# One buffer for a unit's attention data, own output tiles for the W1 jobs, and new ticks for the background jobs

## Chip, core and metric

The kernel runs on one core of one Trainium2 chip. The metric is the device time of one execution in microseconds (us). Before the change three executions took 1047.87, 1049.3 and 1052.65 us; the median is 1049.3 us.

## What is computed

```python
# chunked attention, 4 x 8 heads, 768 tokens, 64 wide; a chunk of 32 queries sees
# 8 memory keys, 16 keys to the left, its own 32 and 8 to the right
out = softmax(q_c @ k_full.T / 8) @ v_full
x = out.transpose(0, 2, 1, 3).reshape(3072, 512)
h = x @ w_in1;  x = (maximum(h, 0) + log1p(exp(-abs(h)))) @ w_out1    # 512 -> 2048 -> 512
h = x @ w_in2;  y = (h - tanh(h)) @ w_out2                            # 512 -> 2048 -> 512
```

All is float32. The kernel splits a float32 operand into a high and a low part and makes three matmuls of one product.

## The kernel before

Tokens come in 24 attention units of 128 and in six blocks of 512. The program has four stages.

1. Opening (to about 125 us). The first weights arrive, units 0 to 7 of the attention and block 0 of the first feed-forward layer run, in an order written out by hand in `OPENING`. There a token such as `L9` loads the score data (`qk`) and values (`v`) of unit 9.
2. Plain blocks (to about 431 us). Blocks 1 to 3 of layer 1 run as products `ff_h` and `ff_y` of twelve matmuls each, 2.72 us a product. After each product `tick()` is called once (L877), and a tick number is the clock of all background work. At the ticks of `ATT_TICKS` (five or six ticks apart) TensorE does, for neighbouring units, the transposes of one (`t_mm`), the value product of the one before (`v_mm`, L371) and the scores of the next (`s_mm`, L290). One tick later (r == 1) SyncE gets the loads of a unit.
3. Phase 0 (ticks 98 to 153, to about 588 us). The last two blocks of layer 1 together, as a fast (Strassen-like) product: seven products in place of eight.
4. Phases 1 to 3, the same form for layer 2. Each phase has an h part of 56 products of six matmuls (1.36 us each; a tick after every second one) and a y part.

In an h part, two lanes alternate: product n belongs to weight group p = 0 or 1 for n = 0 to 13, to p = 2 or 3 for n = 14 to 27, and so on. The weights of a group come from DRAM in a first half (four products, 1024 KB) and a second half (three products, 768 KB), through a ring of five slots (`Ring`, loads at L699). A slot is loaded again once TensorE has made its last product from it, so the load for the second lane's first half (p = 3, 5, 7) can start at the end of n = 6, 20, 34 and is needed at n = 15, 29, 43.

Beside these products run background jobs, started at ticks by tables:

- `JOBS_W1` (16 jobs, `job_w1`): sums of the layer-1 weights for phase 0. A job started at tick t copies the high part on ScalarE at t+2 (L468), stores it at t+3 (`put`, L477), makes the low part on VectorE at t+3 (L472) and stores it at t+4. Each store is 512 KB. The two parts stand in tiles named `o`, a pool of four that is shared with the W2 jobs, the plain output (`out1`, L462) and the x2 jobs.
- `JOBS_W2` (16 jobs (tick, slot, lead), `job_w`): one load of 1024 KB of raw layer-2 weights, and after the lead and four steps of decoding the stores, 768 KB at lead+5 and lead+6 and 1024 KB at lead+8 and lead+9. The first eight are the input weights, the last eight the output weights.
- `JOBS_X` (`job_x`): layer-2 input for the four phases from the layer-1 output: one load of 1024 KB and seven products' inputs, 512 KB each, stored at lead+2 to lead+7.

Every DMA is issued by SyncE in program order. Its queue waits at an instruction whose data, slot or semaphore isn't ready, and all later DMAs wait behind it. `defer` puts a store at the beginning of a later tick, ahead of that tick's attention loads.

Attention tiles `qk` (768 KB) and `v` (512 KB) have two buffers each: at a unit's r == 1 the scores' data of the unit after next are loaded, and the values of the unit itself, which `v_mm` reads two boundaries later.

Of the kernel before, what the change touches and what calls it, by code (L numbers as in the profile page):

```python
# [8 lines left out]
F32 = mybir.dt.float32  # L9
F32R = mybir.dt.float32r  # L10
# [8 lines left out]
B, H, S, D = 4, 8, 768, 64  # L19
NMEM = 8  # L20
CHUNK, LEFT, RIGHT = 32, 16, 8
KEYS = NMEM + LEFT + CHUNK + RIGHT
P = 128
NCH = P // CHUNK
NPAIR = H // 2
# [13 lines left out]
ATT_ORDER = (8, 9, 10, 11, 20, 12, 13, 14, 15, 21, 16, 17, 18, 22, 19, 23)  # L39
ATT_TICKS = (0, 6, 11, 16, 21, 26, 31, 37, 42, 47, 53, 58, 63, 69, 74, 79, 84, 90)  # L40
AT_END = ATT_TICKS[-1]
VIA_DRAM = (20, 21)

# [11 lines left out]
h10 K0 y13 l10 K3 V4 s11 H10 L6 xh4 c47 h11 S5 s13 c19 Y6 K4 mx5 h13 l11 c38 h12 K5 c48 H11 xl4 c110  # L55
l12 c39 K6 y14 l13 ex5 H12 s14 K7 Y7 ml5 c49 T5 c310 Y8 y15 c410 pT5 s15 K8 h14 c111 V5 S6 L7 l14
c311 H13 xh5 h15 mx6 c112 l15 c411 K9 H14 xl5 ex6 c113 K10 Y9 ml6 K11 T6 H15 pT6 c312 c412 K12 V6 S7
xh6 L8 Y10 mx7 ex7 c114 ml7 K13 Y11 xl6 K14 T7 c314 Y12 c313 pT7 c413 c115 V7 Y13 xh7 L9 c315 xl7
c414 c415 K15
"""  # L60
ORDER = "qk0 qk1 qk2 qk3 v0 v1 i0 v2 v3 o0 w1 w2 w3 qk4 v4 w4 w5 w6 w7 qk5 v5 w8 w9 w10 w11 w12 w13 w14 w15"
# [11 lines left out]
HALF = 2 * P  # L73
# [5 lines left out]
AHEAD = 3  # L79
GSLOT = (8, 9, 10, 11, 12, 13, 14, 7)  # L80
JOBS_W1 = (
    (0, "o", 7), (4, "i", 7), (8, "o", 6), (12, "i", 6), (16, "o", 0), (20, "i", 0), (24, "o", 1), (29, "i", 1),
    (35, "o", 2), (40, "i", 2), (44, "o", 3), (48, "i", 3), (52, "o", 4), (61, "i", 4), (70, "o", 5), (75, "i", 5),
)
JOBS_W2 = (
    (5, 15, 3), (17, 15, 3), (23, 6, 3), (31, 15, 3), (38, 6, 3), (46, 15, 3), (51, 6, 3), (60, 15, 3),
    (67, 6, 3), (73, 15, 3), (90, 10, 4), (96, 15, 4), (105, 14, 5), (112, 15, 5), (127, 15, 4), (148, 15, 4),
)
JOBS_X = (
# [3 lines left out]
)  # L93
JOBS_X1 = (79, 91)
# [9 lines left out]
def attention_ffn_ffn(  # L104
# [18 lines left out]
    opool = ctx.enter_context(tc.tile_pool(name="o", bufs=4))  # L123
    attention = ExitStack()
    apool = attention.enter_context(tc.tile_pool(name="a", bufs=2))
# [16 lines left out]
    wid1 = [dpool.tile([P, 7, 2, HALF], F32, name=f"wid1{p}") for p in range(NP)]  # L142
    x1d = dpool.tile([P, KT, len(VIA_DRAM) * P], F32, name="x1d")

# [76 lines left out]
    def run(steps):  # L221
        for _ in steps:
            pass
# [9 lines left out]
    att = {}  # L233

    def qk_load(u):
        t = apool.tile([P, NPAIR * (P + NCH * KEYS)], F32, name="qk")
        nc.sync.dma_start(out=t, in_=qk[u])
        q = t[:, : NPAIR * P].rearrange("p (a t) -> p a t", a=NPAIR)
        k = t[:, NPAIR * P :].rearrange("p (c a k) -> p c a k", c=NCH, a=NPAIR)
        att[u] = dict(q=q, k=k)  # L240
# [16 lines left out]
            nc.scalar.copy(out=out, in_=q)  # L257

    def v_load(u, v=None):
        v = apool.tile([P, NCH, NPAIR, D], F32, name="v") if v is None else v  # L260
        nc.sync.dma_start(out=v.rearrange("p c a d -> p (c a d)"), in_=vv[u])
        att[u]["v"] = v

    def at_load(u):
        qk_load(u)
        v_load(u)
# [72 lines left out]
    def t_mm(u, ps):  # L339
        a = att[u]  # L340
        for p in range(NPAIR):
            nc.tensor.transpose(  # L342
                ps[:, p * P : (p + 1) * P], a["sm"][:, p * P : (p + 1) * P], ident
            )
        a["t"] = ps

    def t_out(u):
        a = att[u]
        if u < UB:
            pT = early[:, UB + u].rearrange("p (a t) -> p a t", a=NPAIR)  # L350
        else:
            pT = apool.tile([P, NPAIR, P], F32, name="pT", bufs=1)
        a["pT"] = pT
        nc.scalar.copy(out=pT.rearrange("p a t -> p (a t)"), in_=a.pop("t"))
# [22 lines left out]
    def x_whole():  # L377
        if "whole" not in xt:
            xt["whole"] = xpool.tile([P, 2, KT, N], F32, name=f"x{PLAIN % 2}")
            n = len(VIA_DRAM) * P  # L380
            nc.sync.dma_start(out=xt["whole"][:, 1, :, :n], in_=x1d)
        return xt["whole"]

    def x_out_whole(u):
        src = att.pop(u)["x"]
        o = (u % UB) * P
        if u in VIA_DRAM:
            x = apool.tile([P, 2 * NPAIR * KEYS], F32, name="sm").rearrange("p (k t) -> p k t", k=KT)
# [3 lines left out]
        yield  # L392
        if u in VIA_DRAM:
            yield
# [68 lines left out]
            nc.vector.tensor_copy(out=o[:, 1], in_=ps_y[e + 2][:, :N])  # L463
            defer(nc.sync.dma_start, y1d[j // 2][e][:, j % 2], o, more=1)

    def split_to(src, dst, shape):
        hi = opool.tile([P, *shape], F32R, name="o")
        nc.scalar.copy(out=hi, in_=src)  # L468
        yield
        put(hi, dst(0))  # L470
        lo = opool.tile([P, *shape], F32R, name="o")
        nc.vector.tensor_tensor(out=lo, in0=src, in1=hi.bitcast(F32), op=ALU.subtract)  # L472
        defer(put, lo, dst(1))

    def put(t, places):
        for at, n, place in places:
            nc.sync.dma_start(out=place, in_=t[:, at : at + n].bitcast(F32))  # L477

    def job_w(kind, p, slot, lead):
# [20 lines left out]
        def place(s, a, n):  # L500
            return wid[p][:, a : a + n, s] if kind == "i" else wod[1][:, a : a + n, p, s]

        yield from split_to(
            w[:, 1:4], lambda s: ((0, 2, place(s, 0, 2)), (2, 1, place(s, 6, 1))), [3, HALF]
        )
        sums(w)
        yield
        yield
        yield from split_to(w, lambda s: ((0, 4, place(s, 2, 4)),), [4, HALF])

    def sums(w, order=(0, 1)):
        add, sub = ALU.add, ALU.subtract
        i, j = order
        nc.vector.tensor_tensor(out=w[:, i], in0=w[:, i], in1=w[:, 3], op=add)
        nc.vector.tensor_tensor(out=w[:, j], in0=w[:, i], in1=w[:, j], op=sub)
        nc.vector.tensor_tensor(
            out=w[:, 2:4], in0=w[:, 2:4], in1=w[:, j : j + 1].to_broadcast([P, 2, HALF]), op=sub
        )
# [11 lines left out]
    def job_w1(kind, p):  # L530
        c = tpool.tile([P, 4, HALF], F32, name="c2", bufs=1)
        a, b = (
            weights["slot", f][:, "io".index(kind)].bitcast(F32).rearrange("p s (i n) -> p i s n", i=2)
            for f in (p, p + NP)
        )
        if kind == "o":
            parts = (c[:, 0:2], a), (c[:, 2:4], b)
        else:
            parts = (c[:, 1:3], a), (c[:, 0:4:3], b)
        for out, x in parts:  # L540
            nc.vector.tensor_tensor(out=out, in0=x[:, :, 0], in1=x[:, :, 1], op=ALU.add)
        yield
        sums(c, (1, 0) if kind == "o" else (0, 1))
        yield

        def place(s):
            return wod[0][:, 2:6, p, s] if kind == "o" else wid1[p][:, 2:6, s]

        yield from split_to(c, lambda s: ((0, 4, place(s)),), [4, HALF])

    def job_x1(half):
        cols = slice(half * N // 2, (half + 1) * N // 2)
# [309 lines left out]
    for t, kind, p in JOBS_W1:  # L862
        plan.setdefault(t, []).append(lambda x=(kind, p): job_w1(*x))
# [7 lines left out]
    place = [0, 0]  # L871
    soft = {}

    def defer(f, *args, more=0):
        late.append((now[0] + more, f, args))

    def tick(chain=iter(())):  # L877
        k = now[0]
        now[0] += 1
        calls, late[:] = [x for x in late if x[0] <= k], [x for x in late if x[0] > k]  # L880
        for _, f, args in calls:
            f(*args)
        if k in starts:
            place[:] = starts[k], k
        i, r = place[0], k - place[1]
        u, done, last = (ATT_ORDER[j] if 0 <= j < len(ATT_ORDER) else None for j in (i, i - 1, i - 2))
        if r == 1 and u is not None:
            if i + 2 < len(ATT_ORDER):
                qk_load(ATT_ORDER[i + 2])
            if i > 1:  # L890
                v_load(u)
            next(soft[u])
        if r == 2 and u is not None:
            run(soft.pop(u))
        if r == 1 and last in VIA_DRAM:
            run(soft.pop(("x", last)))
        if r == 0:
            if done is not None:
                t_mm(done, ps_h[(k // 2 + 1 + k % 2) % 2])
            if last is not None:  # L900
                v_mm(last, ps_a)
            if u is not None:
                s_mm(u, ps_a)
        next(chain, None)
        if r == 0 and done is not None:
            t_out(done)
        next(chain, None)
        if r == 0 and last is not None:
            soft["x", last] = (x_out if last // UB < PLAIN else x_out_whole)(last)
            next(soft["x", last])  # L910
        if r == 0 and u is not None:
            soft[u] = softmax(u)
            next(soft[u])
        if r == 0 and last is not None:
            next(soft["x", last], None)
        run(chain)
        active.extend(job() for job in plan.get(k, ()))
        for job in active[:]:
            if next(job, active) is active:
                active.remove(job)  # L920

    with tc.manual_schedule(engines={mybir.EngineType.PE}):
# [10 lines left out]
        if True:  # L933
# [6 lines left out]
            for name in ORDER.split():  # L940
                kind, i = name.rstrip("0123456789"), int(name.lstrip("qkviow"))
# [23 lines left out]
            for token in OPENING.split():  # L965
                op = token[:2] if token[0] == "c" else token.rstrip("0123456789")
                i = int(token[len(op) :])
# [156 lines left out]
```

## Time and profile before

| | |
|---|---|
| runs, median | 1049.3 us |
| profiled execution | 1051.89 us, its span 1050.1 us |
| TensorE (PE) | 1036.8 us busy, 7327 matmuls |
| VectorE (DVE), ScalarE (ACT) | 766.0 and 620.1 us busy |
| DMA | 319.99 MB, mean 305 GB/s |

The span runs from the first to the last instruction. Busy time of an engine is a sum over the whole span; where TensorE waits, only the waits on it and the chain that ended last can say why.

### The profile page before, as it was taken

The numbers are of one execution on the slowest core, as the hardware profiler recorded it, in microseconds if no ns is written. First come the engines' busy times: TensorE is split into PE (matmuls) and PEld (weight loads), VectorE is DVE, ScalarE is ACT, GpSimd is POOL, SyncE is SP. The second block draws the span as 40 slices with busy tenths as digits, with TensorE's granted clock in tenths as the row PEclk, the third lists the DMA queues.
The fourth block names the chain that finished last, engine by engine and source line by source line (L and its number), as shares of the span: only waits on it lengthen the run. The fifth ranks groups of instructions, "written<-read, shape, count | busy, mean of one in ns | idle before, by whom it ended". The sixth has DMA issues, their size and how long they took to land.

```text
span 1050.1 us, 18534 instructions
## 1 busy us (share of the span) xinstructions
PE 1036.8 (99%) x7327; PEld 848.5 (81%) x7327; DVE 766.0 (73%) x1168; ACT 620.1 (59%) x968; POOL 7.9 (1%) x14
## 2 busy tenths in 40 slices
PE   8999999999999999999999999999999999999998
PEld 5778888888888888877888888888888888888886
DVE  6998467787886774774698687778477777446876
ACT  6998556676675765665664565545455554444553
POOL 2000000000000000000000000000000000000000
PEclk9999999999999999999999999999999999999999
DMA  9989976989898977999999999888799889655661
GB/s 376 407 320 339 294 270 203 318 292 363 296 348 279 340 247 254 376 382 381 331 388 357 341 360 381 303 321 314 264 354 340 320 305 327 213 176 208 239 201 61
DMA packets 112663, 319.99 MB, mean 305 GB/s; under 512 B 8512, under 2 KB 67392, under 8 KB 94144
## 3 DMA queue, kind: packets, MB, share of 16 engines
q1 hardware_dynamic: 112576, 318.80, 84.7%
q8 instruction: 58, 0.95, 0.3%
q14 instruction: 29, 0.24, 0.1%
HBM read 220.73 MB, written 98.04 MB: 304 GB/s over the span
## 4 chain that ended last, share of the span: by engine, by line
PE 88%; DMA 6%; DVE 3%; ACT 2%; issue 1%; SPq 0%; ACTq 0%; DVEq 0%
PE ps_y L408 43%; PE ps_h L408 28%; PE ps_b L408 14%; DMA w<-in_w1i 2%; PE ps_a L371 2%; PE ps_a L290 1%; DMA x<-wid 1%; DMA wod<-o 1%; DMA qk<-in_qk 1%; DVE gl L727 1%; DMA w<-in_qk 1%; PE ps_h L342 1%; DMA wid<-o 1%; DVE o L196 0%; DVE w L727 0%
## 5 line engine op out<-in xcount | busy, mean ns | idle before, releaser
L790 ACT CAST gh<-w 128x512 fp32r<-128x512 f32 x224 | 139.4, 623 | 137.3 <-DVE gl L727 106.8
L727 DVE TENSOR_TENSOR gl<-w,gh 128x512 fp32r<-128x512 f32 x239 | 164.5, 690 | 63.1 <-ACT gh L790 57.0
L408 PE MATMUL ps_h<-x,w 128*128 128x512 f32 x720 | 175.4, 393 | 0.6 <-DVE w L205 0.3
L408 PE MATMUL ps_y<-gh,w 128*128 128x512 f32 x512 | 169.9, 393 | 0.2 <-ACT o L462 0.2
L408 PEld LDWEIGHTS ps_h<-x,w 128*128 128x128 f32 x720 | 133.8, 188 | 31.2 <-DVE w L205 1.5
L408 PE MATMUL ps_y<-w,x 128*128 128x512 f32 x552 | 129.3, 389 | 0.0
L408 PEld LDWEIGHTS ps_y<-w,x 128*128 128x128 f32 x552 | 103.6, 188 | 21.5
L408 PEld LDWEIGHTS ps_y<-gh,w 128*128 128x128 f32 x512 | 96.1, 188 | 21.6 <-ACT o L462 0.6
L408 PE MATMUL ps_y<-gh,x 128*128 128x512 f32 x352 | 109.2, 389 | 0.0
L408 PE MATMUL ps_y<-gl,w 128*128 128x512 f32 x256 | 99.8, 390 | 0.0
L449 DVE TENSOR_TENSOR gl<-t,gh 128x512 fp32r<-128x512 f32 x64 | 45.5, 714 | 52.0 <-ACT gh L444 51.9
L754 ACT ACTIVATE tanh<-sum 128x512 f32<-128x512 f32 x72 | 45.4, 632 | 60.7 <-DVE sum L723 60.5
L408 PEld LDWEIGHTS ps_y<-gh,x 128*128 128x128 f32 x352 | 66.1, 188 | 13.7
L408 PE MATMUL ps_b<-w,x 128*128 128x512 f32 x276 | 71.3, 394 | 0.0
L408 PE MATMUL ps_h<-gh,x 128*128 128x512 f32 x176 | 68.5, 389 | 0.0
L408 PE MATMUL ps_b<-gh,x 128*128 128x512 f32 x176 | 68.5, 389 | 0.0
L408 PE MATMUL ps_y<-gl,x 128*128 128x512 f32 x176 | 68.5, 389 | 0.0
L408 PE MATMUL ps_h<-w,x 128*128 128x512 f32 x252 | 64.5, 391 | 3.0 <-DMA x<-wid 3.0
L432 ACT ACTIVATE t<-ps_h 128x512 f32<-128x512 f32 x64 | 38.1, 597 | 47.7 <-PE ps_h L408 46.8
L727 DVE TENSOR_TENSOR w<-w 128x512 f32<-128x512 f32 x88 | 60.3, 687 | 2.4 <-ACT w L432 1.3
L408 PEld LDWEIGHTS ps_b<-w,x 128*128 128x128 f32 x276 | 52.6, 191 | 11.1
L723 DVE TENSOR_TENSOR sum<-ps_y,kept 128x512 f32<-128x512 f32 x48 | 32.9, 690 | 37.5 <-PE ps_y L408 29.2
(167 smaller groups left out, 1675.3 us busy)
## 6 DMA issues: line engine op xcount, KB each, us to landing
x<-wod SPq DMA_DIRECT2D x44, 1024.0 KB, 5.0
x<-wid SPq DMA_DIRECT2D x27, 1024.0 KB, 7.7
w<-x2d SPq DMA_DIRECT2D x21, 1024.0 KB, 7.3
x<-wid SPq DMA_DIRECT2D x24, 768.0 KB, 7.2
wod<-o SPq DMA_DIRECT2D x32, 512.0 KB, 7.2
wid<-o SPq DMA_DIRECT2D x32, 512.0 KB, 5.7
qk<-in_qk SPq DMA_DIRECT2D x21, 768.0 KB, 6.6
ring<-wod SPq DMA_DIRECT2D x12, 1024.0 KB, 6.6
```

The source lines that it names most:

```text
L290: nc.tensor.matmul(out=ps[cc, j, KEYS * p : KEYS * (p + 1)], lhsT=a["q"][r, p, cc], rhs=a["k"][r, c, p, :], start=True, stop=True,)
L342: nc.tensor.transpose(ps[:, p * P : (p + 1) * P], a["sm"][:, p * P : (p + 1) * P], ident)
L371: nc.tensor.matmul(out=ps[h : h + 64, p % 2, 2 * P + t0 : 2 * P + t0 + CHUNK], lhsT=v, rhs=pT, start=True, stop=True,)
L408: nc.tensor.matmul(out=ps, lhsT=a, rhs=b, start=first and i == 0, stop=last and i == 2, skip_group_check=on,)
L432: nc.scalar.activation(out=out, in_=x, func=AF.Softplus)
L449: eng.tensor_tensor(out=gl, in0=t, in1=gh.bitcast(F32), op=ALU.subtract)
L723: nc.vector.tensor_tensor(out=h, in0=ps, in1=t, op=ALU.add)
L727: nc.vector.tensor_tensor(out=out, in0=x, in1=y, op=ALU.subtract)
L754: nc.scalar.activation(out=t, in_=h, func=AF.Tanh)
L790: nc.scalar.copy(out=gh, in_=src)
```

## The change

The attention tiles lose their second buffer. Units 1, 5 and 7 of the opening use the tiles `oa` and `ob`; all other units use the one `qk` and the one `v`. The loads move one unit nearer to their use: at r == 1 of a unit, the scores' data of the next unit and the values of the unit before. `L9` leaves the opening. When attention's `oa` and `ob` are free (after unit 7), they are the two output tiles of the W1 jobs, which then use none of the four `o` tiles. The three tables get new ticks, slots and leads.

```diff
+AHEAD_UNITS = (1, 5, 7)
-xh6 L8 Y10 ... Y13 xh7 L9 c315 xl7
+xh6 L8 Y10 ... Y13 xh7 c315 xl7
 JOBS_W1 = (
-    (0, "o", 7), (4, "i", 7), (8, "o", 6), (12, "i", 6), (16, "o", 0), (20, "i", 0), (24, "o", 1), (29, "i", 1),
-    (35, "o", 2), (40, "i", 2), (44, "o", 3), (48, "i", 3), (52, "o", 4), (61, "i", 4), (70, "o", 5), (75, "i", 5),
+    (0, "o", 7), (4, "i", 7), (8, "o", 6), (12, "i", 6), (18, "o", 0), (22, "i", 0), (27, "o", 1), (31, "i", 1),
+    (35, "o", 2), (39, "i", 2), (43, "o", 3), (53, "i", 3), (59, "o", 4), (65, "i", 4), (70, "o", 5), (74, "i", 5),
 )
 JOBS_W2 = (
-    (5, 15, 3), (17, 15, 3), (23, 6, 3), (31, 15, 3), (38, 6, 3), (46, 15, 3), (51, 6, 3), (60, 15, 3),
-    (67, 6, 3), (73, 15, 3), (90, 10, 4), (96, 15, 4), (105, 14, 5), (112, 15, 5), (127, 15, 4), (148, 15, 4),
+    (6, 15, 3), (18, 15, 3), (23, 6, 3), (30, 15, 3), (37, 6, 3), (42, 15, 3), (50, 6, 3), (55, 15, 3),
+    (64, 6, 3), (71, 15, 3), (90, 10, 4), (97, 14, 4), (105, 7, 5), (115, 15, 5), (141, 15, 4), (159, 7, 4),
 )
 JOBS_X = (
-    (85, 15, 3, {}), (100, 7, 4, {...}),
-    (155, 7, 5, {...}), (166, 15, 4, {}),
+    (83, 15, 3, {}), (101, 15, 4, {...}),
+    (154, 15, 5, {...}), (166, 15, 4, {}),
@@ qk_load, v_load: one buffer
-        t = apool.tile([P, NPAIR * (P + NCH * KEYS)], F32, name="qk")
+        t = apool.tile(
+            [P, NPAIR * (P + NCH * KEYS)], F32, name="oa" if u in AHEAD_UNITS else "qk", bufs=1
+        )
-        v = apool.tile([P, NCH, NPAIR, D], F32, name="v") if v is None else v
+        if v is None:
+            v = apool.tile([P, NCH, NPAIR, D], F32, name="ob" if u in AHEAD_UNITS else "v", bufs=1)
@@ split_to(src, dst, shape, own=False); job_w1 passes own=True
+            if own:
+                return apool.tile([P, *shape], F32R, name=name, bufs=1)
+            return opool.tile([P, *shape], F32R, name="o")
-        hi = opool.tile([P, *shape], F32R, name="o")
+        hi = tile_of("oa")
-        lo = opool.tile([P, *shape], F32R, name="o")
+        lo = tile_of("ob")
@@ tick
-            if i + 2 < len(ATT_ORDER):
-                qk_load(ATT_ORDER[i + 2])
+            if i + 1 < len(ATT_ORDER):
+                qk_load(ATT_ORDER[i + 1])
             if i > 1:
-                v_load(u)
+                v_load(done)
+        if r == 1 and i == len(ATT_ORDER):
+            v_load(done)
```

## Rows read from the trace of the kernel before

**Rows 1.** Stretches: start:end us, us, busy PE, PEld, DVE, ACT, POOL; granted clock, DMA share, GB/s.
```profile
0.00:100.00 100.00, 93.97 (x1072) 70.27 (x1073) 86.84 (x117) 84.24 (x156) 7.33 (x14) 1.00 0.96 360
100.00:460.00 360.00, 359.79 (x3698) 297.26 (x3697) 261.00 (x412) 231.07 (x310) 0.60 (x1) 1.00 0.87 303
460.00:485.00 25.00, 22.01 (x91) 17.68 (x90) 12.47 (x18) 12.95 (x23) 0.00 (x0) 0.93 1.00 357
485.00:1025.00 540.00, 539.88 (x2380) 446.11 (x2379) 389.68 (x598) 283.27 (x469) 0.00 (x0) 1.00 0.84 304
1025.00:1050.10 25.10, 21.14 (x94) 17.17 (x92) 16.02 (x25) 8.52 (x15) 0.00 (x0) 0.96 0.17 63
```

**Rows 2.** Waits, 125 to 430 us: who <- whom: us in total, times, longest.
```profile
ACT t L432 <- PE ps_h L408: 46.8, 22, 4.5
...
PE ps_y L408 <- ACT o L462: 0.2, 1, 0.2
```

**Rows 3.** TensorE's timeline, 464 to 482 us: start, us, operation [idle before].
```profile
468.91 1.52 PE L408 MATMUL ps_b<-w,x 128*128 128x512 f32 x6
473.43 1.83 PE L408 MATMUL ps_h<-w,x 128*128 128x512 f32 x6 [2.99 <-DMA x<-wid]
...
481.99 0.39 PE L408 MATMUL ps_b<-w,x 128*128 128x512 f32 x1
```

**Rows 4.** The chain that ended last, 451 to 474 us: start, us, what.
```profile
451.46 10.45 DMA wod<-o
...
461.98 0.32 SPq L882
...
462.39 10.99 DMA x<-wid
```

**Rows 5.** SyncE's issues, 407 to 480 us: start, us, line, transfer, count.
```profile
407.87 0.92 SPq L882 DMA_DIRECT2D x2d<-o  x2
...
415.12 10.82 SPq L882 DMA_DIRECT2D x2d<-o  x4
...
479.19 0.55 SPq L482 DMA_DIRECT2D w<-in_w2o  x1
```

**Rows 6.** Two stretches before and in the h part of phase 0; columns as above.
```profile
395.00:410.00 15.00, 15.00 (x67) 12.40 (x67) 7.13 (x11) 6.86 (x13) 0.00 (x0) 1.00 0.53 188
410.00:475.00 65.00, 62.01 (x331) 50.90 (x331) 44.87 (x66) 40.45 (x65) 0.00 (x0) 1.00 1.01 373
```

**Rows 7.** The load issued at 483.55 us: transfer, count, KB, us to landing.
```profile
x<-wid SPq DMA_DIRECT2D x1, 1024.0 KB, 9.6
```

**Rows 8.** TensorE's timeline at 493 us.
```profile
492.87 3.34 PE L408 MATMUL ps_y<-w,x 128*128 128x512 f32 x14
```

**Rows 9.** TensorE's timeline at two attention boundaries.
```profile
159.11 0.86 PE L290 MATMUL ps_a<-qk 64*32 64x64 f32 x64
...
174.19 1.14 PE L371 MATMUL ps_a<-pT,v 64*64 64x32 f32 x64
```

**Rows 10.** SyncE's issues between these boundaries.
```profile
158.22 7.07 SPq L477 DMA_DIRECT2D wod<-o  x2
165.39 0.46 SPq L237 DMA_DIRECT2D qk<-in_qk  x1
165.90 0.94 SPq L261 DMA_DIRECT2D v<-in_vv  x1
```

**Rows 11.** Landing of the loads issued at 165.90 and at 295.59 us.
```profile
v<-in_vv SPq DMA_DIRECT2D x1, 512.0 KB, 7.2
...
v<-in_vv SPq DMA_DIRECT2D x1, 512.0 KB, 10.3
```

**Rows 12.** Landing of W1 stores and others, 125 to 400 us: transfer, count, KB, median us.
```profile
wid<-o SPq DMA_DIRECT2D x32, 512.0 KB, 5.7
```

**Rows 13.** The load issued at 617.27 us, and TensorE's timeline after it.
```profile
x<-wid SPq DMA_DIRECT2D x1, 1024.0 KB, 8.7
...
626.59 12.40 PE L408 MATMUL ps_y<-w,x 128*128 128x512 f32 x54
```

More of the change, by code (lines that the diff above doesn't have):

```diff
@@ L57 @@
 c311 H13 xh5 h15 mx6 c112 l15 c411 K9 H14 xl5 ex6 c113 K10 Y9 ml6 K11 T6 H15 pT6 c312 c412 K12 V6 S7
-xh6 L8 Y10 mx7 ex7 c114 ml7 K13 Y11 xl6 K14 T7 c314 Y12 c313 pT7 c413 c115 V7 Y13 xh7 L9 c315 xl7
+xh6 L8 Y10 mx7 ex7 c114 ml7 K13 Y11 xl6 K14 T7 c314 Y12 c313 pT7 c413 c115 V7 Y13 xh7 c315 xl7
 c414 c415 K15
@@ L464, in out1, with split_to, tile_of @@
             defer(nc.sync.dma_start, y1d[j // 2][e][:, j % 2], o, more=1)
-    def split_to(src, dst, shape):
-        hi = opool.tile([P, *shape], F32R, name="o")
+    def split_to(src, dst, shape, own=False):
+        def tile_of(name):
+            if own:
+                return apool.tile([P, *shape], F32R, name=name, bufs=1)
+            return opool.tile([P, *shape], F32R, name="o")
+        hi = tile_of("oa")
         nc.scalar.copy(out=hi, in_=src)
@@ L547, in place @@
             return wod[0][:, 2:6, p, s] if kind == "o" else wid1[p][:, 2:6, s]
-        yield from split_to(c, lambda s: ((0, 4, place(s)),), [4, HALF])
+        yield from split_to(c, lambda s: ((0, 4, place(s)),), [4, HALF], own=True)
     def job_x1(half):
```

4 rows, old and new, of the table JOBS_X are left out of this document.

## The prediction

> **What bounds the kernel now.** The views were read in this order: stretches, waits, TensorE's timeline at the one wait that matters, the chain back from it, SyncE's issues ahead of it. TensorE sets the time. Its idle time in [rows 1] is 6.0 us in the opening (100 less 93.97), 0.2 us from 100 to 460, 3.0 us from 460 to 485, 0.1 us from there to 1025 and 4.0 us at the end. The change adds and removes no instruction of TensorE, ScalarE or VectorE and no byte of DMA, so it can win only from these gaps and from the clock. The opening waits for the first weights, the tail for the last outputs; neither is moved.
>
> What remains is the 3.0 us. In [rows 3] six matmuls start at 468.91 us; at 1.36 us for six the next should start at 470.27, but start at 473.43, released by a load x<-wid: 3.16 us late. From 473.43 to 481.99 five groups take 8.56 us instead of 6.80: another 1.76 us, in which the granted clock fell below full speed (0.93 over the stretch in [rows 1]; the only other dip is in the tail). The one wait costs 4.92 us.
>
> The reader is to see next why the load came late. By its place in the ring it is p = 5's first half, whose slot was free at about 459.4 us (n = 28 starts at 468.91, so n = 21 started 7 x 1.36 us earlier, and n = 20 was done). SyncE issued it at 462.39, because its queue stood at an earlier store, which itself waited for the landing of a store issued at 451.46 [rows 4]. Then it took 10.99 us. Both delays have one cause: from 410 to 475 us the DMA engines are full (share 1.01, 373 GB/s), while from 395 to 410 they are at 0.53 [rows 6]. So what counts is how many bytes stand ahead of this load since about 410 us.
>
> **The change part by part.**
>
> *Early x2 job, 85 to 83.* Its seven stores (512 KB each) went out two at 407.87, one at 413.34, and four from 415.12 to 425.9 (first and last row of the seven in [rows 5]); the ring's first loads stand between the third and the fourth. Two ticks earlier (5.4 us) five stores stand ahead of the ring loads, and the half empty stretch takes two more of them. That lifts 2 x 0.524 MB, at 373 GB/s 2.8 us, off the full stretch. Bounds: 0 (VectorE is ready no sooner) to 5.6 us (four stores). I take 2.8.
>
> *Second x2 job, 100 to 101, and W2 job, 96 to 97.* The x2 job's store for its third product now comes after the p = 5 load instead of before it: 0.524 MB, 1.4 us. The W2 job's load and first stores still come ahead: 0. Bounds 0 to 2.1 (one more 256 KB store passes). I take 1.4.
>
> Together the load lands 4.2 us earlier, about 469.2 us, against 470.27 needed. The margin of 1.1 us is thin, yet it also can't be issued before 459.4, so it needs a landing in under 10.9 us, as now. Saved: 4.9 us, or 1.7 us less if only one of the two terms comes true.
>
> *W2 job 112 to 115.* Once TensorE doesn't wait, p = 7's first half is needed 4.92 us sooner. Now it is issued at 483.55 and takes 9.6 us, to 493.15 [rows 7]; n = 43 starts 1.36 us after the group at 492.87, at 494.23 [rows 8]: margin 1.1 us. It must land 3.8 us sooner. The W2 load of 1024 KB at 479.19 [rows 5] stands ahead of it and passes behind: 2.8 us; the x2 stores of above are worth 2.8 us here too. 5.6 less 3.8 leaves 1.8 us beside the old 0: cost 0. Without either term it would wait 1 us.
>
> *W2 jobs 127 to 141 and 148 to 159; x2 job 155 to 154.* Phase 0's y part loses the first job and phase 1's h part gets the last one. There p = 5's first half is issued at 617.27 and lands after 8.7 us, at 626.0 [rows 13]; n = 28 starts at 626.59, n = 29 at 627.95: 2.0 us to spare. Bytes ahead of it in that phase: the old job's four stores (1.75 MB) go, the new job's load (1.0 MB) and one x2 store (0.5 MB) come. That is 0.25 MB or 0.7 us less; cost 0, and a wait of the kind above (up to 4.9) if the sum is wrong by 2 us.
>
> *Attention data once.* No load is added: the scores' data wait for the same `s_mm` as before (two buffers and two units ahead name the same release), at the same place of SyncE's queue, and then must land one unit sooner. A five-tick unit: `s_mm` starts at 159.11 and takes 0.86, the next `v_mm` starts at 174.19 [rows 9], so the values have 14.2 us. Where a store of a low part, made on VectorE behind the softmax, stands first in that tick, SyncE gets to them late: the stores from 158.22 hold it until 165.39, 5.4 us after the `s_mm`, and the values leave at 165.90 [rows 10] and land after 7.2 us [rows 11], at 173.1. Even that would be in time, by 1.1 us. By the diff's ticks (t+4 for W1, t+lead+6 and +9 for W2 equal to an attention tick plus one) seven of the five-tick units have such a store now, after ticks 11, 21, 26, 42, 53, 58 and 79. Queued behind it are the two loads and the tick's other stores; TensorE waits for them at the next boundary. With the slow landing of 10.3 us [rows 11], seen where SyncE was not held, each would be 2.0 us late: bounds 0 and 14 us for seven. I take 0.3 us: a held queue lets the engines drain, so 7.2 is the nearer row. L9's removal moves two loads to ticks 1 and 12; TensorE waits 0.2 us in all this stretch, so it can win no more than that.
>
> The Trainium skill ("Trainium Kernel Development and Optimization", Best Practices) says to double-buffer so that DMA and compute overlap, which speaks against this part. By that rule the third rival below is the outcome; here 14.2 us of other matmuls lie between release and use, and no run shows yet that they are enough.
>
> *W1's own tiles.* With one `oa`, the next job's copy waits until the last one's store has landed. The closest jobs are four ticks apart: three ticks, 8.2 us, from store to copy; the median landing is 5.7 us [rows 12]. A landing of 10.3 us would hold ScalarE 2.1 us, and what is queued there first is the softplus; but that waits for TensorE by itself 2.1 us on average (46.8 over 22) [rows 2]. Cost 0, at worst 2 us where both fall together. The plain output no longer shares its tiles with W1 stores: the 0.2 us wait behind it [rows 2] may go. Gain 0.2.
>
> *Ticks of the other W1 and W2 jobs.* The same work, spread differently over ScalarE and VectorE; TensorE waits for neither of them in [rows 1] beyond the 0.2 us. Cost 0; a crowded tick could cost some tenths.
>
> Sum: 1051.89 - 4.9 - 0.2 + 0.3 = 1047.1 us against the profiled execution. That one is 2.6 us above the median of the runs, so 1044.5; for the two thin margins I add 0.3: 1044.8 us.
>
> **The rivals.**
>
> *The wait stays, smaller.* The p = 5 or p = 7 load still misses by 1 to 2 us since full DMA engines take bytes of other jobs instead. For: margins of 1.1 and 1.8 us. Against: 4.2 us of bytes go. Saved then 1 to 3 us: 1046.5 to 1048.5.
>
> *Own tiles hold ScalarE or VectorE.* Stores that land in over 8.2 us in the run of jobs at 27, 31, 35, 39 and 43: four waits of up to 2 us, in part seen by TensorE, while the gain stays: 1045 to 1051, say 1048.
>
> *Single attention buffers make it slower.* TensorE waits at `v_mm` in the held units. It decides at a landing above 8.3 us (1.1 over 7.2) after a held queue. Five to seven waits of 2.0 us, with a clock loss of 1.8 in one or two of them, cost 12 to 17 us: 1055 to 1061 with the gain, say 1056. For: values took 10.3 us at one boundary. Against: not at a held one.
>
> **How the numbers follow.** Forecast 0.56 (1042.5 to 1046.5: all small gaps gone on the one side, two waits under 1 us on the other), wait stays 0.23, own tiles 0.08, slower 0.13. Within 0.5% is about what a measurement of this kernel can tell from no change: 1044.05 to 1054.55 us. The forecast lies 0.75 us above the lower of these bounds and its own range reaches 1.5 us below it; I put 0.36 of all, most from the forecast's 0.56 and a little from the tiles' rival, below the bound: faster 0.36. Of the slow rival 0.11 lie above 1054.55. The same: 0.53. The range 1042 to 1052 leaves out the slow rival and little else.
>
> **What would show it.** Right: no wait x<-wid above 0.5 us, full clock from 460 to 485, idle time between 100 and 1025 under 1 us. Wrong in the first step: an x<-wid wait near 470 or 489. Wrong in attention: rows PE ps_a L371 <- DMA v or L290 <- DMA qk. Wrong in the tiles: ACT o L468 or DVE o L472 <- DMA wid or wod, with PE behind them. If the span drops by much more than 5.2 us, all gaps read here were not the whole.

## The result, and the profile after

The changed kernel takes 1057.4 us (median of five runs, 1055.2 to 1058.6). The kernel before, beside it, takes 1048.0 us (1047.3 to 1052.7). The ratio is 1.0087, with a 95% interval from 1.0071 to 1.0102: it is slower by 9.4 us. The forecast was 1044.8 us. The profiled execution is the one of 1057.43 us; its span is 1055.7 us.

The same stretches as in [rows 1], of the kernel after (the last is longer by 5.6 us):

```profile
0.00:100.00 100.00, 92.44 (x1076) 70.18 (x1077) 87.71 (x117) 84.82 (x156) 7.93 (x14) 1.00 0.96 364
100.00:460.00 360.00, 353.13 (x3662) 291.44 (x3661) 252.10 (x399) 224.12 (x297) 0.00 (x0) 1.00 0.85 296
460.00:485.00 25.00, 25.00 (x112) 20.69 (x111) 18.99 (x28) 15.97 (x26) 0.00 (x0) 1.00 1.01 367
485.00:1025.00 540.00, 537.88 (x2367) 443.15 (x2366) 386.22 (x594) 283.13 (x471) 0.00 (x0) 1.00 0.84 306
1025.00:1055.70 30.70, 26.67 (x118) 21.76 (x116) 20.10 (x32) 11.12 (x19) 0.00 (x0) 1.00 0.24 86
```

The third row is what was forecast: TensorE is busy all of the 25 us at full clock, against 22.01 us and 0.93 in [rows 1]; the product that waited in [rows 3] now starts at 477.61 us, still in this row. The second row is what was not: from 100 to 460 us TensorE now idles 6.9 us, against 0.2 before, and from 485 to 1025 us 2.1 us, against 0.1. The lower busy time of the first row is no loss of this change: the matmuls done by 100 us are about as many (1076 against 1072), and the kernel before, run again (experiment 1), has 91.98 us there.

TensorE's waits in the kernel after, from a view of the whole span, those of the opening left out (who <- whom: us in total, times, longest):

```profile
PE ps_h L346 <- ACT t L436: 3.1, 3, 1.3
PE ps_a L375 <- DMA v<-in_vv: 2.3, 2, 1.2
PE ps_y L412 <- issue: 1.5, 1, 1.5
PE ps_b L412 <- ACT kept L727: 1.3, 2, 0.7
...
PE ps_b L412 <- DVE gl L736: 0.8, 2, 0.7
```

There is no wait x<-wid any more, and none for the plain output as in [rows 2]. The first three rows lie between 125 and 430 us, the last two after 485 us. Line 346 is `t_mm`, the transposes of an attention boundary. They write the bank `ps_h` that the layer's h product has just used, so they can't start before ScalarE's softplus (L436) has read it. That is the largest of the five.

The worst boundary lies at 275 us. TensorE's timeline of the kernel after there, and at 350 us (start, us, operation [idle before]):

```profile
273.85 0.39 PE L412 MATMUL ps_y<-gh,w 128*128 128x512 f32 x1
275.50 0.66 PE L346 MATMUL ps_h<-ident,sm 128*128 128x128 f32 x4 [1.26 <-ACT t L436]
277.38 1.74 PE L375 MATMUL ps_a<-pT,v 64*64 64x32 f32 x64 [1.22 <-DMA v<-in_vv]
...
349.60 0.66 PE L346 MATMUL ps_h<-ident,sm 128*128 128x128 f32 x4 [1.31 <-ACT t L436]
...
356.57 0.39 PE L412 MATMUL ps_y<-gh,w 128*128 128x512 f32 x1 [1.52 <-issue]
```

After two waits of 2.5 us in all, the granted clock falls to 0.50 (1.2 GHz) for 3.4 us from 277.66, another 1.7 us lost (half of 3.4, an estimate).

ScalarE's timeline of the kernel after at the same two places tells what its softplus stood behind:

```profile
273.90 1.05 ACT L477 CAST oa<-c 128x1024 fp32r<-128x1024 f32 x1 [1.47 <-DVE c L525]
274.85 0.59 ACT L436 ACTIVATE t<-ps_h 128x512 f32<-128x512 f32 x1
...
346.91 1.21 ACT L495 ACTIVATE w<-w,low_bias 128x1024 uint32<-128x1024 uint32 x1 [4.51 <-DMA w<-in_w2o]
348.02 1.03 ACT L477 CAST oa<-c 128x1024 fp32r<-128x1024 f32 x1
348.95 0.59 ACT L436 ACTIVATE t<-ps_h 128x512 f32<-128x512 f32 x1
```

At 273.90 a W1 job's high copy into `oa` waited 1.47 us for VectorE's sums, while the softplus, whose product had ended at 271.5, stood behind it. At 346.91 a W2 job's first decode waited 4.51 us for its raw load; the copy and the softplus came behind that.

The values come late twice. The chain of waits of the kernel after up to the first time (start, us, what):

```profile
236.22 7.37 DMA wid<-o
...
243.60 14.85 DMA v<-in_vv
```

SyncE's issues of the kernel after ahead of both:

```profile
238.94 2.25 SPq L215 DMA_DIRECT2D w<-w1d  x2
241.29 0.89 SPq L891 DMA_DIRECT2D y1d<-o  x2
242.24 0.42 SPq L491 DMA_DIRECT2D w<-in_w2i  x1
...
243.60 0.41 SPq L265 DMA_DIRECT2D v<-in_vv  x1
...
267.66 0.36 SPq L486 DMA_DIRECT2D wid<-ob  x1
268.12 0.46 SPq L240 DMA_DIRECT2D qk<-in_qk  x1
268.62 0.88 SPq L265 DMA_DIRECT2D v<-in_vv  x1
```

The first time 2 MB of w1d loads, 1 MB of y1d stores and a W2 job's 1 MB go out within 5 us ahead of the values, with 768 KB of scores' data between, which take 14.85 us; [rows 11] had 7.2 and 10.3. The second time SyncE's queue is held by a low part's store until 267.66, and the values leave only at 268.62 and land 8.7 us later.

### The profile page after: what moved, and what is told of

It reads as the page before. It is cut to its first block, busy times and chain, and to the rows that moved or that the text cites. A ratio compares the mean times of both kernels' runs of the same rounds, so it can differ in the third digit from the quotient of the medians.

```text
span 1055.7 us, 18528 instructions
## 1 busy us (share of the span) xinstructions
PE 1035.1 (98%) x7327; PEld 847.2 (80%) x7327; DVE 765.1 (72%) x1168; ACT 619.2 (59%) x968; POOL 7.9 (1%) x14
## 4 chain that ended last, share of the span: by engine, by line
PE 79%; DMA 9%; DVE 6%; ACT 3%; issue 2%; SPq 0%; ACTq 0%; DVEq 0%
PE ps_y L412 39%; PE ps_h L412 24%; PE ps_b L412 12%; DMA v<-in_vv 2%; DMA w<-in_w1o 2%; PE ps_a L375 2%; PE ps_a L294 1%; DMA x2d<-w 1%; DVE gl L736 1%; DMA w<-in_w2o 1%; DMA x2d<-gh 1%; DMA w<-in_qk 1%; DVE o L197 1%; DMA wid<-o 1%; DVE o L481 1%
## 5 line engine op out<-in xcount | busy, mean ns | idle before, releaser
L436 ACT ACTIVATE t<-ps_h 128x512 f32<-128x512 f32 x64 | 38.0, 596 | 42.0 <-PE ps_h L412 41.1
```

Source lines behind the costliest of these rows:

```text
L436: nc.scalar.activation(out=out, in_=x, func=AF.Softplus)
```

## Experiments

Times are medians; ratios, with their 95% intervals, are to the kernel before, run beside each.

**1 to 4: which part.** The kernel before again; the kernel before with all three new tables (two buffers, shared tiles); the kernel after with the old tables; the kernel after with W1's tiles taken from the shared `o`.

```diff
 # 1: the kernel before, unchanged
 # 2: the kernel before
-JOBS_W1, JOBS_W2, JOBS_X = (old ticks)
+JOBS_W1, JOBS_W2, JOBS_X = (new ticks)
 # 3: the kernel after
-JOBS_W1, JOBS_W2, JOBS_X = (new ticks)
+JOBS_W1, JOBS_W2, JOBS_X = (old ticks)
 # 4: the kernel after
-        yield from split_to(c, ..., [4, HALF], own=True)
+        yield from split_to(c, ..., [4, HALF])
```

Expected of 1: 

> The kernel before once more, nothing changed: a second profile of it. The wait of 3.0 us on x<-wid at 470 us cost 4.9 us in the first profile (1051.89 us), but the median of its runs is 1048.0 us. If the wait belongs to this kernel, this profile shows it again (span about 1050 us). If it comes in some executions only, the profile has a span of about 1045 to 1046.5 us and no wait above 0.5 us between 100 and 1025 us, and the change had no 4.9 us to win in most runs.

Expected of 2: 

> The kernel before with the new tables of W1, W2 and x2 jobs alone (two attention buffers, shared output tiles). If the new ticks are what costs (W2 loads that land after their decode's tick, W2 jobs inside the later h parts: 3.2 us there alone), this run is 5 to 10 us slower than before. If the single attention buffers or the own tiles cost, it is within 3.5 us of before, and what remains is the 3.2 us of the later phases.

Expected of 3: 

> The changed kernel with the old tables: one attention buffer, own W1 tiles, L9 gone, old ticks. If the single buffers cost by themselves, TensorE waits at v_mm for v<-in_vv in two or more units and the run is 4 to 9 us slower than before. If they cost only together with the new ticks, no such wait is above 0.5 us and the run is within 2 us of before. If the own tiles alone cost, ScalarE waits for the landing of an oa store for over 2 us and a transpose group on TensorE waits for a softplus behind it.

Expected of 4: 

> The changed kernel with W1 outputs in the shared o tiles again: new ticks and one attention buffer. ScalarE's wait of 4.2 us for an oa store at 256 us is gone by construction. If that wait is the root of the waits at 274 to 278 us (3.9 us with the clock), the run is 4 us faster than the changed kernel, about 1053. If the ticks and the buffers are the root, it is within 1.5 us of the changed kernel.

Measured: 1 takes 1048.2 us (1.0002 [0.9988, 1.0016]), 2 takes 1059.2 us (1.0094 [1.0066, 1.0122]), 3 takes 1047.5 us (0.9990 [0.9977, 1.0003]), 4 takes 1061.6 us (1.0120 [1.0090, 1.0150]). So the ticks alone make all of the loss, and the tiles by themselves none of it. Run 4 came out above the kernel after, where the expectation had it at or below. It differs from 2 in attention's buffers (and `L9`) alone: with the new ticks the single buffers cost 2.4 us by the medians, though the two intervals overlap.

TensorE's waits from 100 to 1025 us in 1, the kernel before once more (span 1046.7 us):

```profile
PE ps_h L408 <- DMA x<-wid: 1.4, 1, 1.4
PE ps_y L408 <- DMA x<-wid: 0.6, 1, 0.6
PE ps_y L408 <- ACT o L462: 0.4, 1, 0.4
```

This shows what the forecast was built on: the wait of 2.99 us with its clock loss [rows 3] is that of one execution, a long one. Here the same wait is 1.4 us and costs no clock. Of 112 runs of the kernel before in these comparisons, 10 took between 1051.5 and 1053.8 us, like the profiled one (1051.89); the rest took 1046.7 to 1050.5. By this second profile there were mostly some 2 us to be had, not 4.9.

The same view of 2, the new ticks with the old buffers:

```profile
PE ps_h L342 <- ACT t L432: 3.8, 4, 2.0
PE ps_y L408 <- ACT o L462: 3.7, 2, 3.1
```

The waits of the transposes are there without any change of buffers; waits for values aren't. With shared tiles the plain output waits too (3.7 us here, 3.1 us in 4), with W1's own tiles it doesn't: they help the new ticks.

The same view of 3, the new buffers with the old ticks (span 1045.6 us):

```profile
PE ps_y L412 <- DMA x<-wid: 0.7, 1, 0.7
PE ps_h L412 <- DMA x<-wid: 0.5, 1, 0.5
```

There is no wait for values or scores: with the old ticks one buffer is enough. 3 and the kernel after differ in the tables alone, and their spans by 10.1 us. TensorE's waits make 9.0 - 1.2 = 7.8 us of that and the half clock 1.7; 0.6 us are left over.

**5 to 8: which table.** Each is number 3 with one part of the new tables.

```diff
 # 5: all W1 ticks of after
 # 6: the first ten W2 jobs of after
 # 7: the last six W2 jobs and the x2 jobs of after, and (73, 15, 3) at 72
 # 8: as 7, but W2 at 130 and 148 and the third x2 job at 155: JOBS_X, JOBS_W2
-(85, 15, 3), (100, 7, 4)
+(83, 15, 3), (101, 15, 4)
-(73, 15, 3), (90, 10, 4), (96, 15, 4), (105, 14, 5), (112, 15, 5), (127, 15, 4), (148, 15, 4)
+(72, 15, 3), (90, 10, 4), (97, 14, 4), (105, 7, 5), (115, 15, 5), (130, 15, 4), (148, 15, 4)
```

Expected of 5: 

> e3_tiles (1047.45 us) with the new W1 ticks alone. If the W1 ticks cost by themselves (runs of jobs four ticks apart, copies that wait for sums), TensorE's waits between 220 and 361 us (7 us and more in the changed kernel) come back: 1052 us or more. If only the early W2 ticks cost, it is within 1.5 us of 1047.5. If the two cost together and not alone, both this run and the next are within 2 us and their sum doesn't explain the changed kernel.

Expected of 6: 

> e3_tiles with the ten early W2 ticks alone (6, 18, 23, 30, 37, 42, 50, 55, 64, 71). If these loads are the cause (issued at ticks 37 and 42 ahead of the attention loads, at 64 behind block ends, decoded three ticks later by a ScalarE that then waits for the landing), the wait of ScalarE for w<-in_w2o near 345 us (4.5 us) and a late softplus come back: 1051 us or more. Else within 1.5 us of 1047.5.

Expected of 7: 

> e3_tiles with the new late W2 ticks and the new x2 ticks alone (one early W2 job at 72 in place of 73, since its slot is wanted at 83). The changed kernel gains about 2 us at 470 to 500 us over the kernel before and loses about 2.5 us at 580 to 675 us. If both come from these tables, the run is within 1 us of 1047.5, without the waits on x<-wid and with waits on kept and gl near 588 and 656 us.

Expected of 8: 

> e3_tiles with only those of the late ticks that my prediction counted on: x2 jobs at 83 and 101, W2 jobs at 97, 105 (slot 7), 115; the last ones at 130 and 148, x2 at 155. If the byte sum is right, the waits on x<-wid (0.55 and 0.70 us in e3_tiles) are gone and nothing is lost later: 1046.2 us, about 1.3 us under e3_tiles. If the h part is bound by VectorE and ScalarE too, new waits on kept or gl take its place and it stays at 1047 to 1048.

Measured: 5 takes 1056.6 us (1.0087 [1.0072, 1.0103]), 6 takes 1050.2 us (1.0022 [1.0012, 1.0033]), 7 takes 1049.6 us (1.0016 [1.0002, 1.0031]), 8 takes 1047.4 us (1.0000 [0.9990, 1.0009]). The W1 ticks alone bring as much as the whole change; the parts don't add up (8.7 + 2.2 + 1.6 thousandths against 8.7).

TensorE's waits from 100 to 1025 us in 5, its two longest rows:

```profile
PE ps_h L346 <- ACT t L436: 3.8, 1, 3.8
PE ps_h L412 <- DMA x<-wid: 1.1, 1, 1.1
```

The same view of 7:

```profile
PE ps_b L412 <- ACT kept L727: 0.8, 2, 0.7
PE ps_b L412 <- DVE gl L736: 0.8, 2, 0.7
```

In 8 the stretch of [rows 1]'s third row:

```profile
460.00:485.00 25.00, 25.00 (x112) 20.54 (x111) 17.54 (x27) 16.01 (x27) 0.00 (x0) 1.00 1.02 372
```

In 5 one wait of 3.8 us ends at 278 us, with the clock at half from 276.3 to 283.1 us. Five of these 6.8 us are work, so an estimated 2.5 us are lost by it; wait and clock make 6.3 of the 8.6 us by which the span of 5 exceeds that of 3. In 6 no softplus is late, and its loss lies between the two expected ones; its longest wait is one of 1.1 us for values. In 7 and 8 the x<-wid waits are gone, as forecast; 7 gives this back in phases 0 and 1 by two waits of 0.7 us, at 581 and 649 us, which 8 without the late jobs (ticks 141, 159, 154) doesn't have. 8 also confirms the count of bytes: five x2 stores go out ahead of the ring's first loads where three did, the load of [rows 4] is issued at 460.35 us and lands after 8.0 us, at 468.4, and the product that needs it starts at 469.67 without a wait. And it shows how little there was: it idles 0.35 us from 100 to 1025 us, its span is 1045.0 us against 1046.7 in 1 and 1045.6 in 3, and its time is that of the kernel before. The gain of 1.3 us over 3 that was expected doesn't show in the medians (1047.4 against 1047.5 us), and no new waits explain that.

**9 to 12: which W1 jobs.**

```diff
 # 9: number 3 with two W1 jobs a tick earlier
-(40, "i", 2), (44, "o", 3)
+(39, "i", 2), (43, "o", 3)
 # 10: number 3 with all W1 ticks of after but these two
 # 11: number 9 with the raw load of a W2 job two ticks earlier, its steps where they were
-(38, 6, 3)
+(36, 6, 5)
 # 12: the kernel after with these two back
-(39, "i", 2), (43, "o", 3)
+(40, "i", 2), (44, "o", 3)
```

Expected of 9: 

> e3_tiles (old tables, 1047.45 us) with two W1 jobs one tick earlier and nothing else: 40 to 39 and 44 to 43. In e5_w1 one wait of 3.8 us before a transpose group at 278 us, with 1.4 us of clock, came at the boundary after these two jobs. If these two ticks are its cause, this run has the wait again and is 5 to 7 us slower than e3_tiles. If it needs the jobs before them (27 and 31 in place of 24 and 29), it is within 1.5 us of e3_tiles.

Expected of 10: 

> The counterpart: all new W1 ticks but these two, which stay at 40 and 44, on e3_tiles. If the pair is the cause, about 1049.5 us (e5_w1's 1056.6 less the 6.5 us between 260 and 285 us). If the other moved jobs are, 1054 us or more.

Expected of 11: 

> e9_pair with the raw load of one W2 job two ticks earlier and the job's steps where they were (38 with lead 3 becomes 36 with lead 5). In e5_w1 ScalarE stood 2.8 us at 257 us for the landing of this load, 14.0 us after its issue, with the W1 copy and the softplus queued behind it. If this landing is the trigger, most of what e9_pair loses is won back (to within 2 us of e3_tiles). If the crowding of steps on VectorE and ScalarE at this boundary is, it stays within 1.5 us of e9_pair.

Expected of 12: 

> The changed kernel (1057.4 us) with the two W1 jobs back at 40 and 44. There the waits from 256 to 278 us cost 5.7 us in the profile, behind a 4.2 us wait of ScalarE for an oa store. If the pair is the cause there too, 1052 us or less. If the new W2 ticks (37 and 42 beside them) keep that stretch late, it stays above 1055 us.

Measured: 9 takes 1052.7 us (1.0028 [1.0009, 1.0047]), 10 takes 1051.9 us (1.0032 [1.0019, 1.0044]), 11 takes 1052.5 us (1.0035 [1.0021, 1.0048]), 12 takes 1054.6 us (1.0056 [1.0036, 1.0076]). The pair makes a wait of 2.9 us of the transposes, at 275 us, and between a third (by the ratios) and a little under half (by the medians) of what all W1 ticks cost in 5. The earlier load of 11 took away ScalarE's wait of 1.4 us for it, and the transposes still waited 2.6 us: the load isn't the cause. In 10 the same wait is 1.4 us, with one of 0.8 us for values. But there the softplus stands not behind a W1 copy but behind a W2 job's cast, which VectorE's decoding (L503) let start 2.6 us after the h product's end, against 1.2 us in 3. So the other W1 ticks act in another way, perhaps through VectorE; that isn't shown. 10 and 12 both lie between the two times that were expected of them: the pair is part of the loss, in the kernel after 2.8 of 9.4 us by the medians.

**13 to 16: which of the pair, and why.** 13 and 14 move one job each. 15 and 16 leave the sums early and put only the high copy (with what follows it) a tick later: in 15 for the job of tick 39, in 16 for all sixteen jobs of the kernel after.

```diff
 # 13: number 3
-(40, "i", 2)
+(39, "i", 2)
 # 14: number 3
-(44, "o", 3)
+(43, "o", 3)
 # 15: number 9; 16: the kernel after, without the condition
         sums(c, (1, 0) if kind == "o" else (0, 1))
         yield
+        if (kind, p) == ("i", 2):
+            yield
```

Expected of 13: 

> The kernel after with the old tables, but the W1 job of tick 40 starts at 39. Theory A (the job's high copy now falls one tick earlier, on ScalarE ahead of the softplus whose bank the boundary's transposes at about 275 us need, and the copy waits for VectorE's sums): this one job carries the loss of the pair, 1051.5 to 1053.5 us with a wait of the transposes on the softplus of 2 to 3.5 us near 275 us. Theory B (the two jobs crowd VectorE together): half of it, 1049.5 to 1050.5 us. Theory C (the job of tick 44 did it): as before, about 1047.5 us.

Expected of 14: 

> The kernel after with the old tables, but the W1 job of tick 44 starts at 43. Theory A: as before, 1047 to 1048.5 us, no wait of the transposes above 0.5 us. Theory B: 1049.5 to 1050.5 us. Theory C: 1051.5 to 1053.5 us.

Expected of 15: 

> The pair at 39 and 43, and in the job of tick 39 the high copy (with the subtraction and the two stores behind it) one tick later than its sums, so that ScalarE makes it behind the softplus of the boundary's bank; the sums stay early. Theory A (order in ScalarE's queue): the wait of the transposes near 275 us is under 0.5 us and the time 1047 to 1049 us. Theory B (VectorE is crowded by the early sums): the softplus still comes late, 1051 to 1053 us.

Expected of 16: 

> The kernel after, with one tick more between sums and high copy in all sixteen W1 jobs. Theory A: copies find their sums made, so waits of the softplus behind a copy go; but a copy may fall ahead of another boundary's softplus, and the waits for values and for the late W2 and x2 jobs stay: 1053 to 1056 us. Theory B (early sums, early W2 steps): as after, 1056.5 to 1058.5 us. As bad as after or worse would also fit A only if the trace shows new waits of the same kind at other boundaries.

Measured: 13 takes 1049.0 us (1.0008 [0.9997, 1.0019]), 14 takes 1052.4 us (1.0036 [1.0025, 1.0048]), 15 takes 1052.2 us (1.0034 [1.0022, 1.0045]), 16 takes 1063.6 us (1.0142 [1.0121, 1.0163]). I had the wrong job: the one at 44 does it (theory C). So 15 delayed a copy that costs little, and says nothing on the mechanism. 16, slower than the times given for either theory, loses the wait at 275 us and gets worse ones. TensorE's waits from 100 to 1025 us in 16:

```profile
PE ps_h L346 <- ACT t L436: 3.8, 1, 3.8
PE ps_a L375 <- DMA v<-in_vv: 3.6, 2, 2.8
```

ScalarE's timeline of 16 ahead of the first, at 355 us:

```profile
353.75 1.23 ACT L495 ACTIVATE w<-w,low_bias 128x1024 uint32<-128x1024 uint32 x1 [7.93 <-DMA w<-in_w2o]
354.85 0.60 ACT L436 ACTIVATE t<-ps_h 128x512 f32<-128x512 f32 x1
```

Here it is a W2 job's decode that stands ahead of the softplus and waits 7.93 us for its load. Each boundary has its own neighbours: one tick for all copies only moves the waits.

**17 and 18: the copy of the right job.**

```diff
 # 17: number 14; 18: the kernel after
         yield
+        if (kind, p) == ("o", 3):
+            yield
```

Expected of 17: 

> The kernel after with the old tables, the W1 job of tick 44 started at 43 as in the run before, its sums early, but its high copy (with the subtraction and the stores behind it) put back to the old tick 46. Theory A (the copy's place in ScalarE's queue, ahead of the softplus that the boundary's transposes wait for, is what costs): no wait of the transposes above 0.7 us near 275 us, and 1047 to 1049 us. Theory B (the early sums on VectorE are what costs): the wait of 2.9 us stays, 1051.5 to 1053 us.

Expected of 18: 

> The kernel after, with only that one job's high copy (started at tick 43) one tick later. Theory A: the wait of the transposes and its half clock at 274 to 278 us go, worth 1.4 to 2.6 us, so 1054.5 to 1056 us; the other waits of the kernel after stay. Theory B: as after, 1057 to 1058.5 us.

Measured: 17 takes 1047.9 us (0.9996 [0.9986, 1.0006]), 18 takes 1056.7 us (1.0076 [1.0059, 1.0093]). The timeline of 14 at the boundary, ScalarE's rows with TensorE's h product and transposes, and one later wait of TensorE:

```profile
267.50 2.88 PE L412 MATMUL ps_h<-x,w 128*128 128x512 f32 x12
...
271.86 0.90 ACT L477 CAST o<-w 128x768 fp32r<-128x768 f32 x1 [2.25 <-DVE w L503]
274.36 1.04 ACT L477 CAST oa<-c 128x1024 fp32r<-128x1024 f32 x1 [1.59 <-DMA wid<-oa]
275.31 0.59 ACT L436 ACTIVATE t<-ps_h 128x512 f32<-128x512 f32 x1
...
275.95 0.66 PE L346 MATMUL ps_h<-ident,sm 128*128 128x128 f32 x4 [2.85 <-ACT t L436]
...
475.59 1.66 PE L412 MATMUL ps_h<-w,x 128*128 128x512 f32 x6 [1.90 <-DMA x<-wid]
```

The same of 17:

```profile
267.42 2.88 PE L412 MATMUL ps_h<-x,w 128*128 128x512 f32 x12
...
272.03 0.90 ACT L477 CAST o<-w 128x768 fp32r<-128x768 f32 x1 [2.25 <-DVE w L503]
272.82 0.59 ACT L436 ACTIVATE t<-ps_h 128x512 f32<-128x512 f32 x1
...
273.47 0.66 PE L346 MATMUL ps_h<-ident,sm 128*128 128x128 f32 x4 [0.45 <-ACT t L436]
...
274.29 1.05 ACT L477 CAST oa<-c 128x1024 fp32r<-128x1024 f32 x1 [0.23 <-DMA wid<-oa]
...
470.44 1.66 PE L412 MATMUL ps_h<-w,x 128*128 128x512 f32 x6 [0.53 <-DMA x<-wid]
```

Both start the job's sums at tick 43; in 17 the copy comes behind the softplus, and the softplus starts 2.5 us earlier. The wait goes from 2.85 to 0.45 us, and with it the half clock: by the start of the next y product (282.59 against 278.80 us) the boundary costs 3.7 us less. The time goes from 1052.4 to 1047.9 us. Not all of that is the boundary: in the two profiles the wait for x<-wid at 475 and 470 us makes another 1.4 us. That wait varies between profiles (1.5 to 1.9 us in 9, 10, 11 and 14, 0.3 to 0.6 in 3, 13, 15 and 17), and no run shows what sets it. The early sums of theory B stay in 17 and the wait is gone, so the mechanism at this boundary is theory A's, for the job at 44. The edit also puts back the subtraction and the stores behind the copy; the wait of the softplus, though, is seen in ScalarE's own rows. The 0.45 us that remain stand behind the W2 job's cast, which starts 1.7 us after the h product's end here and 1.2 us in 3, where nothing waits: that much may be the early sums' part. What the copy itself waited for differs: VectorE's sums in the kernel after, the store of `oa` in 14. Its place ahead of the softplus is what costs in both.

The Trainium skill ("PSUM — Partial Sum Buffer", Engine vs sequencer instructions) calls the queues of ScalarE and VectorE strictly first in, first out. The trace agrees: in 14 the softplus started at 275.31, behind the cast and the copy, while the product it reads had ended at 270.4, some 5 us earlier.

In 18 the same edit wins only 0.8 us, its interval overlapping that of the kernel after; 1054.5 to 1056 us had been expected. TensorE's timeline in 18:

```profile
275.10 0.60 PE L346 MATMUL ps_h<-ident,sm 128*128 128x128 f32 x4
278.46 1.27 PE L375 MATMUL ps_a<-pT,v 64*64 64x32 f32 x64 [2.76 <-DMA v<-in_vv]
```

The transposes of this boundary don't wait any more (at three others they still do), but the values, issued late behind the held queue, are what is late next: 2.76 us in place of 1.26 + 1.22, and the half clock stays.

No version is clearly faster than the kernel before: 3, 8 and 17 take 1047.4 to 1047.9 us.

## Why the prediction was wrong, point by point

- *What bounds the kernel now.* Right that TensorE sets the time and that only gaps can be won. The size of the main gap was taken from one execution: 4.92 us there, 2.0 us in the profile of experiment 1. The sum then went down by another 2.6 us, from the profiled execution to the median. But by experiment 1 the profiled execution is long because of this very wait, so the same time was taken off twice; in the kernel's usual executions the gain forecast wasn't there.
- *Early x2 job; second x2 job and W2 job; W2 job 112 to 115.* The mechanism was right: no x<-wid wait is left in the kernel after, nor in 7 and 8. By 8 it wins 1.7 us of span against 1, 0.6 us against 3 and, by the medians, nothing that can be measured. One margin was misread: an issue at 459.4 and a landing "as now", 10.99 us, would still have missed 470.27; in 8 the landing fell to 8.0 us.
- *W2 jobs 127 to 141 and 148 to 159; x2 job 155 to 154: cost 0.* Wrong by about 2 us: 7 against 8 is 1049.6 against 1047.4 us. Only the bytes ahead of one load were counted; the waits that came are on ScalarE's copies `kept` and VectorE's low parts `gl`, two engines that the late W2 jobs use too. That these jobs delay them is argued from 7 against 8, not traced.
- *Attention data once: 0.3 us.* With the old ticks right: 3 has no wait for values, and 1047.5 us. The Trainium skill ("Trainium Kernel Development and Optimization", Best Practices) wants two buffers so that DMA and compute overlap. 3 has one, shows no wait for values and a ratio of 0.9990: here other matmuls cover the load. With the new ticks it was short: two waits of 1.1 and 1.2 us. The second came as the third rival said, a held queue and a landing of 8.7 us, above the 8.3 at which it was to decide. But two buffers with the same ticks (2) lose as much, so this rival isn't the main cause; by 4 against 2 it is worth some 2 us. That the measured 1057.4 us lies in this rival's range, 1055 to 1061, is luck for the most part.
- *W1's own tiles: cost 0, gain 0.2.* Right in sign, too small: 4 without them takes 1061.6 us, about 4 us more than the kernel after. A copy did wait 4.2 us for a store of `oa`, from 256.6 us on, but TensorE did not wait for the softplus behind it; in 14 such a store held the copy for 1.59 us ahead of the softplus, the second rival's way, and there TensorE did wait.
- *Ticks of the other W1 and W2 jobs: "Cost 0; a crowded tick could cost some tenths".* This is the step that failed. The W1 ticks alone cost 8.5 us and the early W2 ticks 2.2. The reason given was that TensorE waits for neither ScalarE nor VectorE in [rows 1]. That says that the old order had no job that delayed an urgent instruction, and nothing of another order. What the runs showed in its place: a background step ahead of the softplus makes the boundary's transposes wait. The room can be worked out from the rows: between the h product and the transposes TensorE makes a y product of 2.72 us, and the softplus takes 0.59, so it may start some 2.1 us after the h product has ended. It started 2.5 us after it in 17, 3.3 in the kernel after, 4.9 in 14 and 5.9 in 5; the waits were 0.45, 1.26, 2.85 and 3.81 us, each what exceeds the 2.1. In 3, with the old ticks, it started 2.0 us after it and TensorE didn't wait: the old order had 0.1 us to spare at this place, and an added copy of 1.05 us with its own wait could not fit.
- What stays open: the 1.5 us at 356.57 in the kernel after, for which the trace names no releaser (2, 4, 5, 6, 10 and 18 have one too, of 0.3 to 1.3 us); the shares of the remaining W1 jobs in 10's loss, which were not tried one by one; and the waits of the kernel after at other places, whose causes are read from the trace and were not removed by an edit. Moving the one copy in the kernel after won only 0.8 us of 9.4.

## What to carry to other kernels

Where the bound engine idles only a few microseconds, a new order of background work has little to win and can lose at every in-order queue. For each moved step, look at which urgent instruction it now stands in front of, how much room that instruction has, and what the step itself waits for. Read a wait that is to be removed in more than one execution before it is counted as a gain. Where two resources are late at one place, taking away one wait gives back only the difference between them (18).

## What the runs showed of the hardware

- Short idle times of TensorE were followed by a lower granted clock: after 2.99 us of waiting (before) it was 0.50 for 3.3 us, after 2.85 us (14) and 2.5 us in two pieces (after) 0.50 for 3.4 us; with 3.81 us (5) it was 0.50 for 6.8 us, which began inside the wait. After 1.90 us (14, at 475 us), 1.37 us (1) and 0.45 us (17) it stayed at 1.00.
- A 512 KB load that was issued within 5 us after some 4 MB of other transfers and 768 KB more took 14.85 us to land; with the queue held before it, 8.7 us.
- Executions of the same program differ: of 112 runs of the kernel before, 10 took 1051.5 to 1053.8 us, the others 1046.7 to 1050.5. In the one profile of the first kind a wait for a load was 1.6 us longer than in the one of the second, and the clock fell behind it; that the other long runs have the same reason isn't shown.
